# A whole order by hand: five engines in written order, later q casts on POOL, v loads issued by ACT, layer norm in three items

## The chip, the cores and the metric

The kernel runs on one core of a Trainium2 chip. The metric is the device time of one execution in microseconds (us). The engines are PE (TensorE, matrix products), DVE (VectorE), ACT (ScalarE), POOL (GpSimd) and SP (SyncE, here only a DMA issuer). Times of one kernel spread by some 3%. The sets of runs were made on different chips, so a kernel is compared with the kernel before of its own set. A run over 1.5% above the fastest of its kernel in the same set counts as slow and is left out of the ratios. The ratios are the mean time of one kernel's fast runs over that of the other's fast runs of the same rounds, so they are not quite the ratio of the medians that stand beside them. Verdicts use a line of 2%.

## The reference

A decaying linear attention feeds a gated MLP. Shapes: q, k, v are 4 x 8 x 768 x 64 (batch, head, position, head dimension); the MLP has 512 inputs and 1024 hidden values, half gate and half content.

```python
# attention, per batch and head, in blocks of 64 positions
intra = ((q_b @ k_b.T) * Dmask) @ v_b              # Dmask: lam^(i-j) for i >= j
inter = (q_b * lam_pow) @ kv_state
out[block] = intra + inter
kv_state = lam_block * kv_state + (k_b * rev_pow).T @ v_b
# gated MLP on x = out, heads side by side
h = relu(x @ w_in);  u, v = h[..., :512], h[..., 512:]
v_n = (v - mean(v)) / sqrt(var(v) + 1e-6)           # over the last axis
v_s = w_spatial @ v_n + b_spatial[:, None]          # mixes the 768 positions of a batch
y = (u * v_s) @ w_out
```

Each batch can start its spatial product (`w_spatial @ v_n`) only when the attention and the layer norm of all its positions are done. That product is what the text calls **pvs**; the first pvs of each batch is a good milestone.

## The kernel before

The work is cut into 12 steps of 256 positions, three steps for each of the four batches. One step n consists of these items:

```python
load_step(n)   # k, q, v of the step from memory, all issued by SP
cast_step(n)   # kd = k * decay (DVE for n < 3, else POOL); qc = q (ACT); vc = v (POOL); all to bf16
trans_step(n)  # T: PE transposes kd and qc; ACT copies kT, DVE writes qT
scores_step(n) # A: PE scores pam; DVE multiplies the mask: a
kv_step(n)     # K: PE state update pkv; DVE s = decay * s_prev + pkv (through a tile sd)
out_step(n)    # O: PE output pat = state part + a @ v; ACT copies to xT
pv(b, r)       # content half of w_in; relu on ACT (vh); layer norm on DVE and ACT (vn)
pu(b, r)       # gate half of w_in; relu on ACT (uT)
pvs(b, f), po(b, r)   # spatial product and gate; output product and store
```

The order of PE's and POOL's instructions is written by hand. DVE, ACT and SP are ordered by the framework's scheduler. The hand-written loop looks ahead: while step n is put out, step n + 1 is scored, step n + 2 is cast and transposed, and the MLP's products are put between as fill, so that PE has independent work while DVE and ACT finish a link of the attention.

```python
    with tc.manual_schedule(engines={PE, mybir.EngineType.Pool}):
        # ... cast_step(0), win, cast_step(1), spatial and output weights, trans, scores, kv of step 0, trans of step 1
        for n in range(NS):
            if n + 2 < NS:
                cast_step(n + 2)
            if n + 5 < NS:
                load_step(n + 5)
            if n + 1 < NS:
                scores_step(n + 1)
            out_step(n)
            after_out(n)                 # appends pv, pu, pvs, po to the list of fills
            if n + 1 < NS:
                kv_step(n + 1)
            f = fills.get(n, 4 + (n % 3 == 0))
            fill(f // 2)
            if n + 2 < NS:
                trans_step(n + 2)
            fill(f - f // 2)
        fill(len(pend))
```

Of the kernel before, what the change touches and what calls it, by code (L numbers as in the profile page):

```python
# [9 lines left out]
FP32 = mybir.dt.float32  # L10
BF16 = mybir.dt.bfloat16
I32 = mybir.dt.int32
AF = mybir.ActivationFunctionType
ALU = mybir.AluOpType
PE = mybir.EngineType.PE
# [3 lines left out]
def kernel(  # L19
# [12 lines left out]
    nc = tc.nc  # L32
    P = 128
    B, H, S, D = q.shape
    DM = H * D
    DFF = moe_w_in.shape[1]
    DH = DFF // 2
    NBLK = S // P
    NG = H // 2
    NCH = DM // P  # L40
# [16 lines left out]
        return psum.tile(shape, dt, tag="ps", name=name)  # L57


    lam_bc = const.tile([P, H], FP32)  # L60
    nc.scalar.dma_start(out=lam_bc, in_=lam.unsqueeze(0).to_broadcast((P, H)))

    st = {}

    def load_step(n):
        b, r = divmod(n, NR)
        toks = slice(r * T2, (r + 1) * T2)
        q_in = fin.tile([P, H, 2, D], FP32, tag="q_in", name=f"q_in_{n}")
        k_in = fin.tile([P, H, 2, D], FP32, tag="k_in", name=f"k_in_{n}")
        v_in = fin.tile([P, H, 2, D], FP32, tag="v_in", name=f"v_in_{n}")  # L70
        for c in range(2):
            nc.sync.dma_start(out=k_in[:, :, c, :],  # L72
                              in_=k[b, :, toks][:, c * P:(c + 1) * P].rearrange("h p d -> p h d"))
        nc.sync.dma_start(out=q_in.rearrange("p h m d -> p h (m d)"),  # L74
                          in_=q[b, :, toks].rearrange("h (p m) d -> p h (m d)", m=2))
        for c in range(2):
            nc.sync.dma_start(out=v_in[:, :, c, :],  # L77
                              in_=v[b, :, toks][:, c * P:(c + 1) * P].rearrange("h p d -> p h d"))
        st[n] = {"q_in": q_in, "k_in": k_in, "v_in": v_in}

    load_step(0)
    ident = const.tile([P, P], BF16)
    make_identity(nc, ident)

    def iota_f(shape, pattern, base, mult, name):
        ti = const.tile(shape, I32, name=name + "_i")
        nc.gpsimd.iota(ti, pattern=pattern, base=base, channel_multiplier=mult)
        tf = const.tile(shape, FP32, name=name)
        nc.vector.tensor_copy(out=tf, in_=ti)
        return tf  # L90

    krev = iota_f([P, 1], [[0, 1]], P - 1, -1, "krev")

    qpos = iota_f([P, 2, 2, D], [[1, 2], [0, 2], [2, D]], 1, 0, "qpos")

    rel = iota_f([P, 2, D], [[1, 2], [2, D]], 0, -1, "rel")

    win_sb = wpool.tile([P, NCH, DFF], BF16)
    wout_sb = wpool.tile([P, NCH, DM], BF16)
    bsp_bc = wpool.tile([P, S], BF16)  # L100
    wt_sb = wpool.tile([P, NBLK, S], BF16)
    wsp_raw = wpool.tile([P, NBLK, S], BF16)

    def load_win(f0, f1):
        nc.gpsimd.dma_start(out=win_sb[:, :, f0:f1],
                            in_=moe_w_in.rearrange("(g p) f -> p g f", p=P)[:, :, f0:f1])

    load_win(DH, DFF)
    for n in range(1, 4):
        load_step(n)  # L110


    loglam = const.tile([P, H], FP32)
    nc.scalar.activation(out=loglam, in_=lam_bc, func=AF.Ln)
# [3 lines left out]
        nc.vector.tensor_copy(out=logl[rows, :], in_=loglam[rows, hh::2])  # L118
    ldec = const.tile([P, H], FP32)
    nc.scalar.activation(out=ldec, in_=loglam, func=AF.Exp, scale=krev[:, 0:1])  # L120
    lq = const.tile([P, NG, T2], BF16)
    for g in range(NG):
        nc.scalar.activation(out=lq[:, g, :], in_=qpos.rearrange("p m a d -> p (m a d)"),
                             func=AF.Exp, scale=logl[:, g:g + 1])
    l128 = const.tile([P, NG], FP32)
    nc.scalar.activation(out=l128, in_=logl, func=AF.Exp, scale=float(P))
    lm128 = const.tile([P, H], FP32)
    nc.scalar.activation(out=lm128, in_=loglam, func=AF.Exp, scale=-float(P))
    causal = const.tile([P, P], FP32)
    nc.vector.tensor_scalar(out=causal, in0=rel.rearrange("p m d -> p (m d)"), scalar1=0.0,  # L130
                            scalar2=None, op0=ALU.is_ge)
    amask = const.tile([P, 2, 2, 2, P], FP32)
    for h in range(H):
        nc.vector.tensor_scalar(out=amask[:, h // 4, h % 2, (h // 2) % 2, :], in0=causal,
                                scalar1=lm128[:, h:h + 1], scalar2=None, op0=ALU.mult)
    eps_t = const.tile([P, 1], FP32)
    nc.vector.memset(eps_t, 1e-6)
    oo128 = const.tile([P, P], BF16)
    nc.vector.memset(oo128, 1.0 / P)


    xT = {}

    def cast_step(n):
        s = st[n]
        kd = att.tile([P, 2, H, D], BF16, tag="kd", name=f"kd_{n}")
        qc = att.tile([P, 2, H, D], BF16, tag="qc", name=f"qc_{n}")
        vc = att.tile([P, H, 2, D], BF16, tag="vc", name=f"vc_{n}")
        eng = nc.vector if n < NR else nc.gpsimd
        eng.tensor_tensor(out=kd.rearrange("p c h d -> p h c d"), in0=s["k_in"],  # L150
                          in1=ldec.unsqueeze(2).unsqueeze(3).broadcast_to((P, H, 2, D)),
                          op=ALU.mult)
        nc.scalar.activation(out=qc.rearrange("p m h d -> p h m d"), in_=s["q_in"], func=AF.Copy)  # L153
        nc.gpsimd.tensor_copy(out=vc, in_=s["v_in"])  # L154
        s["kd"], s["qc"], s["vc"] = kd, qc, vc

# [112 lines left out]
    def pv(b, r):  # L269
        if r == 0:  # L270
            gmlp_tiles(b)
        x, m = xT[b], gm[b]
        vh, mv, rstd = m["vh"], m["mv"], m["rstd"]
        ps = two_banks([P, 2, DH], f"pv_{b}_{r}")
        for j in range(2):
            for c in range(NCH):
                nc.tensor.matmul(out=ps[:, j], lhsT=x[:, r, c, j * P:(j + 1) * P],  # L277
                                 rhs=win_sb[:, c, DH:DFF], start=(c == 0), stop=(c == NCH - 1))
        pair = slice(2 * r, 2 * r + 2)
        nc.scalar.activation(out=vh[:, pair, :], in_=ps, func=AF.Relu)  # L280
        for t in (2 * r, 2 * r + 1):
            nc.vector.bn_stats(out=m["st6"][:, t, :], in_=vh[:, t, :])  # L282
            nc.vector.bn_aggr(out=mv[:, t, :], in_=m["st6"][:, t, :])
        nc.scalar.activation(out=rstd[:, pair], in_=mv[:, pair, 1], func=AF.Sqrt,
                             bias=eps_t[:, 0:1])
        nc.vector.reciprocal(out=rstd[:, pair], in_=rstd[:, pair])
        for t in (2 * r, 2 * r + 1):
            nc.vector.tensor_scalar(out=m["vn"][:, t, :], in0=vh[:, t, :],  # L288
                                    scalar1=mv[:, t, 0:1], scalar2=rstd[:, t:t + 1],
                                    op0=ALU.subtract, op1=ALU.mult)  # L290
# [45 lines left out]
        nc.scalar.activation(out=wt_sb[:, s:s + 2, :], in_=ps[:, :, 0:S], func=AF.Copy)  # L336


    pend = []

    def fill(n):
        for _ in range(min(n, len(pend))):
            pend.pop(0)()

    def after_out(n):
        b, r = divmod(n, NR)
        pend.append(lambda: pv(b, r))
        if r == 0:
            pend.append(lambda: pu(b, 0))
        if r == NR - 1:  # L350
            pend.append(lambda: pu(b, 1))
            pend.append(lambda: pu(b, 2))
            if b == 0:
                pend.extend([lambda s=s: wt_piece(s) for s in (0, 2, 4)])
            pend.extend([lambda f=f: pvs(b, f) for f in range(NCH)])
            pend.extend([lambda i=i: po(b, i) for i in range(NR)])

    with tc.manual_schedule(engines={PE, mybir.EngineType.Pool}):
        cast_step(0)
        load_win(0, DH)  # L360
        cast_step(1)
        nc.gpsimd.dma_start(out=wsp_raw, in_=moe_w_spatial.rearrange("(a p) s -> p a s", p=P))
        nc.gpsimd.dma_start(out=bsp_bc, in_=moe_b_spatial.unsqueeze(0).to_broadcast((P, S)))
        nc.gpsimd.dma_start(out=wout_sb, in_=moe_w_out.rearrange("(t p) f -> p t f", p=P))
        trans_step(0)
        scores_step(0)
        kv_step(0)
        trans_step(1)
        load_step(4)
        fills = {0: 1, 1: 2, 2: 5}  # L370
        for n in range(NS):
            if n + 2 < NS:
                cast_step(n + 2)
            if n + 5 < NS:
                load_step(n + 5)
            if n + 1 < NS:
                scores_step(n + 1)
            out_step(n)
            after_out(n)
            if n + 1 < NS:  # L380
                kv_step(n + 1)
            f = fills.get(n, 4 + (n % 3 == 0))
            fill(f // 2)
            if n + 2 < NS:
                trans_step(n + 2)
            fill(f - f // 2)
        fill(len(pend))


# [28 lines left out]
```

## Time and profile before

| | before |
|---|---|
| time, median (range) of 3 runs | 188.25 us (187.67 to 188.35) |
| span of the profiled run | 186.7 us |
| PE busy, idle | 145.7, 41.0 us |
| DVE, ACT, POOL busy | 103.4, 89.1, 34.8 us |
| first pvs of the four batches at | 63.7, 102.1, 136.8, 166.0 us |

The page's first part gives busy time, share and instruction count of each engine. Its row PEclk gives the clock granted to TensorE in 40 slices of the span, in tenths:

```profile
PE 145.7 (78%) x1540; PEld 96.5 (52%) x1540; DVE 103.4 (55%) x191; ACT 89.1 (48%) x98; POOL 34.8 (19%) x35
PEclk9999996975999979999999999999999999999999
```

PE's clock falls in slices 6 to 14 only (counted from 0), that is before 70 us. The view of waits lists what an engine waited for (us in total, times, longest). Its first lines for PE are the holes of the first stage:

```profile
PE pt L163 <- DVE kd L150: 15.5, 2, 14.3
PE pkv L207 <- POOL vc L154: 8.1, 1, 8.1
```

The first is the start, before any data is there. The second is the wait for v of step 2.

### The profile page before, as it was taken

What the parts mean: (1) busy time and instruction counts of PE and PEld (TensorE: products, weight loads), DVE (VectorE), ACT (ScalarE), POOL (GpSimd) and SP (SyncE); (2) the same over time, 40 slices, a digit from 0 to 9 for tenths busy, and PEclk for the clock granted to TensorE, in tenths of its full rate; (3) what the DMA queues carried; (4) which work ended last, traced back from release to release, by engine and by line L of the source; (5) the groups of instructions that cost most, each with busy time, mean ns of one, the idle gap of its engine ahead of it and who ended that gap; (6) DMA issues with size and microseconds to landing.
All of it is one profiled execution on the core that took longest, in us unless ns stands there. A gap on an engine that the chain in (4) does not pass through costs nothing.

```text
span 186.7 us, 3638 instructions
## 1 busy us (share of the span) xinstructions
PE 145.7 (78%) x1540; PEld 96.5 (52%) x1540; DVE 103.4 (55%) x191; ACT 89.1 (48%) x98; POOL 34.8 (19%) x35
## 2 busy tenths in 40 slices
PE   0005677507979779999997999999799999999980
PEld 0005563305649556655776665575676646565430
DVE  1029993705399853542989747169884722564400
ACT  4244324712677942268775613666722157660051
POOL 4004060006245344060606005020000000000000
PEclk9999996975999979999999999999999999999999
DMA  4999969999999999999998900530000027000035
GB/s 98 218 211 252 205 161 184 199 212 232 199 241 248 200 239 238 221 225 222 330 254 195 252 8 0 208 133 4 0 0 4 2 79 262 0 0 4 0 132 205
DMA packets 68337, 28.36 MB, mean 152 GB/s; under 512 B 50528, under 2 KB 65248, under 8 KB 68320
## 3 DMA queue, kind: packets, MB, share of 16 engines
q1 hardware_dynamic: 65664, 25.17, 56.5%
q0 software_dynamic: 2512, 2.95, 9.6%
q8 instruction: 12, 0.20, 0.5%
q14 instruction: 5, 0.04, 0.1%
q10 hardware_dynamic: 144, 0.00, 0.0%
HBM read 24.78 MB, written 6.29 MB: 166 GB/s over the span
## 4 chain that ended last, share of the span: by engine, by line
PE 54%; SPq 13%; DVE 11%; ACT 9%; DMA 9%; issue 2%; POOL 1%; ACTq 0%; POOLq 0%
PE pvs L307 17%; PE po L322 11%; DMA v_in<-in_v_dram 9%; PE pv L277 8%; PE pu L297 7%; SPq L77 6%; SPq L72 5%; PE pt L163 4%; DVE a L192 3%; PE pvs L309 3%; SPq L74 3%; DVE st L282 3%; ACT vh L280 2%; ACT wt_sb L336 2%; DVE vn L288 2%
## 5 line engine op out<-in xcount | busy, mean ns | idle before, releaser
L307 PE MATMUL pvs<-wt_sb,vn 128*128 128x384 bf16 x192 | 37.8, 331 | 2.1 <-ACT wt_sb L336 2.0
L192 DVE TENSOR_TENSOR a<-pam,amask 128x1024 bf16<-128x1024 f32 x24 | 28.5, 1210 | 6.0 <-PE pam L189 6.0
L154 POOL CAST vc<-v_in 128x1024 bf16<-128x1024 f32 x12 | 12.9, 1074 | 84.0 <-DMA v_in<-in_v_dram 42.7
L252 ACT ACTIVATE xT<-pat 128x1024 bf16<-128x1024 f32 x12 | 15.8, 1320 | 23.7 <-PE pat L249 23.6
L307 PEld LDWEIGHTS <-vn 128*128 128x128 bf16 x192 | 18.9, 99 | 14.9 <-issue 2.5
L297 PE MATMUL pu<-xT,win_sb 128*128 128x256 bf16 x192 | 24.4, 285 | 1.9 <-DVE a L192 1.9
L311 DVE TENSOR_TENSOR gT<-pvs,uT 128x768 bf16<-128x768 f32 x16 | 15.3, 958 | 18.2 <-PE pvs L309 18.1
L277 PE MATMUL pv<-win_sb,xT 128*128 128x512 bf16 x96 | 24.2, 400 | 1.2 <-ACT xT L252 1.2
L322 PE MATMUL po<-wout_sb,gT 128*128 128x512 bf16 x96 | 21.9, 379 | 1.5 <-DVE a L192 1.1
L297 PEld LDWEIGHTS <-win_sb 128*128 128x128 bf16 x192 | 19.2, 102 | 5.7 <-issue 1.8
L153 ACT ACTIVATE qc<-q_in 128x1024 bf16<-128x1024 f32 x12 | 12.7, 1055 | 19.0 <-DMA q_in<-in_q_dram 19.0
L325 ACT ACTIVATE o<-po 128x1024 f32<-128x1024 f32 x12 | 12.3, 1025 | 19.0 <-PE po L322 19.0
L282 DVE BATCH_NORM_STATS2 st<-vh 128x6 f32<-128x512 bf16 x24 | 15.6, 682 | 10.4 <-ACT vh L280 10.3
L163 PE MATMUL pt<-ident,kd 128*128 128x128 bf16 x96 | 8.6, 242 | 15.5 <-DVE kd L150 15.5
L170 DVE TENSOR_TENSOR qT<-pt,lq 128x1024 bf16<-128x1024 bf16 x12 | 8.2, 684 | 18.5 <-ACT kT L168 18.5
L150 POOL TENSOR_TENSOR kd<-k_in,ldec 128x1024 bf16<-128x1024 f32 x9 | 17.1, 1897 | 6.1 <-DMA k_in<-in_k_dram 6.1
L168 ACT ACTIVATE kT<-pt 128x1024 bf16<-128x1024 bf16 x12 | 12.2, 1021 | 11.2 <-PE pt L163 11.2
L280 ACT ACTIVATE vh<-pv 128x1024 bf16<-128x1024 f32 x12 | 12.3, 1024 | 8.8 <-PE pv L277 8.8
L163 PEld LDWEIGHTS <-kd 128*128 128x128 bf16 x96 | 7.2, 110 | 17.4 <-DVE kd L150 15.7
L277 PEld LDWEIGHTS <-xT 128*128 128x128 bf16 x96 | 9.5, 102 | 11.7 <-issue 1.7
L322 PEld LDWEIGHTS <-gT 128*128 128x128 bf16 x96 | 9.2, 98 | 11.9 <-issue 1.0
L299 ACT ACTIVATE uT<-pu 128x1024 bf16<-128x1024 f32 x12 | 12.2, 1020 | 5.9 <-PE pu L297 5.8
(52 smaller groups left out, 146.2 us busy)
## 6 DMA issues: line engine op xcount, KB each, us to landing
k_in<-in_k_dram SPq DMA_DIRECT2D x24, 256.0 KB, 5.8
q_in<-in_q_dram SPq DMA_DIRECT2D x12, 512.0 KB, 6.1
v_in<-in_v_dram SPq DMA_DIRECT2D x24, 256.0 KB, 6.0
out_dram<-o SPq DMA_DIRECT2D x12, 512.0 KB, 3.4
wsp_raw<-in_moe_w_spatial_dram POOLq DMA_DIRECT2D x1, 1152.0 KB, 11.3
win_sb<-in_moe_w_in_dram POOLq DMA_DIRECT2D x2, 512.0 KB, 8.4
wout_sb<-in_moe_w_out_dram POOLq DMA_DIRECT2D x1, 512.0 KB, 14.8
bsp_bc<-in_moe_b_spatial_dram POOLq DMA_DIRECT2D x1, 192.0 KB, 11.7
```

The source lines that it names most:

```text
L150: eng.tensor_tensor(out=kd.rearrange("p c h d -> p h c d"), in0=s["k_in"], in1=ldec.unsqueeze(2).unsqueeze(3).broadcast_to((P, H, 2, D)), ...
L154: nc.gpsimd.tensor_copy(out=vc, in_=s["v_in"])
L163: nc.tensor.transpose(out=pt[:, j, g, c * P:(c + 1) * P], in_=src[:, c, 2 * g:2 * g + 2, :].rearrange("p h d -> p (h d)"), identity=ident)
L192: nc.vector.tensor_tensor(out=a_sb[:, i].rearrange("p h g c x -> p (h g) c x"), in0=pam.rearrange("p h g c x -> p (h g) c x"), in1=amask[: ...
L252: nc.scalar.activation(out=xT[b][:, r].rearrange("p g (c d m) -> p (g c) m d", c=2, m=2), in_=po.rearrange("p g c (m d) -> p (g c) m d", m ...
L277: nc.tensor.matmul(out=ps[:, j], lhsT=x[:, r, c, j * P:(j + 1) * P], rhs=win_sb[:, c, DH:DFF], start=(c == 0), stop=(c == NCH - 1))
L280: nc.scalar.activation(out=vh[:, pair, :], in_=ps, func=AF.Relu)
L282: nc.vector.bn_stats(out=m["st6"][:, t, :], in_=vh[:, t, :])
L297: nc.tensor.matmul(out=ps[:, f], lhsT=win_sb[:, c, f * P:(f + 1) * P], rhs=x[:, r, c, :], start=(c == 0), stop=(c == NCH - 1))
L307: nc.tensor.matmul(out=ps[:, i, 0:HW_], lhsT=m["vn"][:, s, f * P:(f + 1) * P], rhs=wt_sb[:, s, cols], start=(s == 0), stop=False)
L311: nc.vector.tensor_tensor(out=m["gT"][:, f, :].rearrange("p (i x) -> p i x", i=2), in0=ps[:, :, 0:HW_], in1=m["uT"][:, f, :].rearrange("p ...
L322: nc.tensor.matmul(out=ps[:, j], lhsT=gT[:, c, t * P:(t + 1) * P], rhs=wout_sb[:, c, :], start=(c == 0), stop=(c == NCH - 1))
```

## The change

The intent is a front without the hole at v of step 2 and full control of what runs when. All five engines follow one hand-written text of items. v goes out on ACT's hardware queue, so that it need not queue behind k and q; the weights go out one after another when they are needed; q casts of steps 3 and up go to POOL; layer norm is split into l0 (statistics, DVE), l1 (square root, ACT) and l2 (reciprocal and vn, DVE), which can be placed apart.

```diff
+    def load_v(n):
         for c in range(2):
-            nc.sync.dma_start(out=v_in[:, :, c, :], ...
+            nc.scalar.dma_start(out=v_in[:, :, c, :], ...
+    ctx.enter_context(tc.manual_schedule(engines={
+        PE, mybir.EngineType.Pool, mybir.EngineType.Activation, mybir.EngineType.DVE,
+        mybir.EngineType.SP}))
+    for n in range(4):
+        load_step(n)                     # k and q of four steps first on SP
+    load_v(0)                            # ... load_v(1) follows the tables on ACT
 ...
-        nc.scalar.activation(out=qc.rearrange("p m h d -> p h m d"), in_=s["q_in"], func=AF.Copy)
+        if n == 0:
+            nc.vector.tensor_copy(out=qo, in_=s["q_in"])
+        elif n < NR:
+            nc.scalar.activation(out=qo, in_=s["q_in"], func=AF.Copy)
+        else:
+            nc.gpsimd.tensor_copy(out=qo, in_=s["q_in"])
 ...
-    # the loop with lookahead and fills
+    run("""
+        c:0 win T:0 mask A:0 K:0 O:0 pv:0:0 l0:0:0 pu:0:0 l1:0:0
+        c:1 lv:2 T:1 l2:0:0 A:1 K:1 O:1
+        c:2 wsp lv:3 T:2 pv:0:1 pu:0:1 l0:0:1 l1:0:1 A:2 l2:0:1 K:2 O:2
+        wout lk:4 c:3 lv:4
+        pv:0:2 l0:0:2 pu:0:2 wt:0 l1:0:2 wt:2 l2:0:2 wt:4
+        lk:5 c:4 lv:5 T:3 pvs:0:0 pvs:0:1 A:3 K:3 lk:6 c:5 lv:6 pvs:0:2 T:4 pvs:0:3 po:0:0
+        A:4 O:3 K:4 po:0:1 lk:7 c:6 lv:7 T:5 po:0:2 pv:1:0
+        ...
+    """)
+    for n in range(2 * NR, NS):          # a = batch before that of step n
+        run(f"A:{n + 1} O:{n} K:{n + 1}")            # guards left out
+        if r == 0:
+            run(f"l2:{a}:2 pvs:{a}:0 pvs:{a}:1 {nxt} pvs:{a}:2 pvs:{a}:3")
+        ...
```

Each engine takes its instructions in the order of this text. `T:1` stands for the transposes of step 1, `l2:0:1` for the normalization of the second third of batch 0, `lk` and `lv` for the loads.

## The prediction

> **What bounds the kernel now.** I first read the page's slices, then the chain of waits that ended last, then the timeline of the first 60 us, and last the busy time by stretch.
>
> ```profile
> PE   0005677507979779999997999999799999999980
> DMA  4999969999999999999998900530000027000035
> ```
> One digit is 4.67 us. TensorE (PE) is full from about slice 15 (70 us) on; before that it has holes, while the DMA engines are full. So there are two stages. The table by stretch (columns: stretch, its length, busy us and instructions of PE, PEld, DVE, ACT and POOL, granted PE clock, DMA share, GB/s) puts numbers on them:
> ```profile
> 35.00:40.00 5.00, 0.02 (x2) 0.00 (x0) 2.40 (x5) 2.89 (x3) 0.00 (x0) 1.00 1.19 202
> 60.00:70.00 10.00, 7.47 (x104) 5.59 (x102) 7.22 (x9) 7.49 (x7) 3.48 (x3) 0.86 1.12 219
> 90.00:100.00 10.00, 9.38 (x119) 6.76 (x117) 9.29 (x24) 7.93 (x11) 2.87 (x3) 1.00 1.08 273
> 140.00:150.00 10.00, 9.63 (x105) 6.04 (x103) 5.92 (x7) 2.33 (x2) 0.00 (x0) 1.00 0.01 2
> ```
> Adding PE's column over the stretches: 37.7 us busy in 0 to 70 (32.3 idle), 106.5 in 70 to 180 (3.5 idle), 1.5 in the last 6.7 (5.2 of tail: last copy, last store). Only the first stage has much to give. The chain of waits (start, us, what) names its largest piece:
> ```profile
> 25.91 15.96 DMA v_in<-in_v_dram
> 41.91 0.08 issue
> 42.00 1.05 POOL vc L154
> 43.09 0.43 PE pkv L207 x6
> ```
> PE stood still because the state update of step 2 waited for v of step 2. The timeline shows what that load ran beside:
> ```profile
> 25.44 0.83 POOL L362 DMA_DIRECT2D wsp_raw<-in_moe_w_spatial_dram  x1
> 26.26 0.56 POOL L363 DMA_DIRECT2D bsp_bc<-in_moe_b_spatial_dram  x1
> 26.54 10.03 SPq L72 DMA_DIRECT2D k_in<-in_k_dram  x2
> 26.81 0.76 POOL L364 DMA_DIRECT2D wout_sb<-in_moe_w_out_dram  x1
> 42.00 1.04 POOL L154 CAST vc<-v_in 128x1024 bf16<-128x1024 f32 x1 [14.43 <-DMA v_in<-in_v_dram]
> 43.09 0.43 PE L207 MATMUL pkv<-vc,kd 128*64 128x64 bf16 x8 [8.07 <-POOL vc L154]
> ```
> Spatial weights, bias and output weights (1152 + 192 + 512 KB as landed) went out at 25.4 to 27.6 and landed 11.3 to 14.8 us after issue (page, DMA issues). From 26 to 42 the DMA moved about 3.1 MB at 177 to 243 GB/s, of which those weights are 1.9 MB; v of step 2 got through at 41.9. None of them is used before 59. The v load is also last in SP's queue, behind k and q of its step and backpressure of up to 10 us for two issues.
>
> [...] So v on ACT's queue [...] lets v pass the k and q queued ahead. [...] two vn took 2.09 us at 44.09 beside a POOL kd of 1.90 at 43.81, and 0.73 for two at 54.68 with POOL idle. [...] granted clock 0.50 in 30 to 32; eight pv took 3.57 us at 29.76, 1.89 at 47.72. [...] for vc, 1.04 us; I take 1.05 for a qc cast there.
>
> **The change, part by part.**
> Steady state. PE's work is unchanged. From the warm pieces of the chain, one step costs transposes 0.89 + scores 0.55 + attention output 1.13 + state 0.25 + pv 1.73 + pu 1.85 = 6.40; a batch adds pvs, four tiles of 2 x (0.97 + 0.16) = 9.04, and po 3 x 1.73 = 5.19. A batch is 33.4. Before, first po to first po takes 34.76 and 34.57 us (79.82, 114.58, 149.15), so it idles 1.2 a batch; hand ordering can save at most some 3.5 us there, and I credit none.
> Casts: 9 x 1.06 = 9.5 us leave ACT for POOL, whose step becomes 1.90 + 1.05 + 1.04 = 4.0 of about 11.5 us; both lie beside PE. Cost: [...] up to about 1 us of DVE delay a step, mostly hidden as DVE is 55% busy.
> v issues: 24 move from SP to ACT. An unobstructed SP issue took 0.43 us, the obstructed ones up to 5.10. About 1 us a step on ACT cancels the cast gain; hidden later, dangerous in the first 30 us.
> Layer-norm pieces as separate items: same instructions, other places in the queues, no work removed. Early Sqrt table: the 1.28 us load at 36.4 moves to the start.
> Front. I lay it out anew; estimates from durations above:
> - k0, q0 (SP) and v0 (ACT) are 1.57 MB. With data from about 2.3 us at 215 GB/s, v0 lands near 7, q0 near 10. Before, the first win half shared this time and the first transposes began at 14.33. Now: qc on DVE to 11, transposes (cold) 11 to 13, kT 1.02, qT 0.69, scores, mask 1.66 and two a of 1.2 in a row, output and xT 1.3: xT at about 20.5. Before it was 27.3: 7 us sooner.
> - win is issued by POOL only after v0's cast, at about 9 to 10.5; its halves took 8.1 and 8.7 us alone, so both land near 18 and 24. pv of step 0 runs 20.5 to 24 and pu 24 to 27.5, cold. So late win costs little.
> - ACT then does uT, sqrt, qc1 to about 29, and issues v2. Step 1: transposes 30, kT, qT, scores 32.5, a, output, xT at 35.5; v2, issued 29 to 30 and alone with SP at half of 215 GB/s, needs 4.9 us and lands about 35. POOL casts it and issues the spatial weights at 36.5.
> - Step 2: cast 36.5, transposes, pv and pu of step 1 to 41, scores, output, xT at 44.5; pv, pu of step 2 to 48; spatial weights land 36.5 + 11.3 = 48; wt pieces and evictions (1.46 each) to 53.
> - So the first pvs starts at about 53 instead of 66.49. But before had by then also done the attention of step 3 and the scores of step 4, some 4 us of PE, which after still owes.
> Sum: 53 + first batch's pvs and po 14.2 + 3 x 33.4 + idle 3 x 1.2 + tail 5.2 = 176.2. Span to reported time adds 1.6 (188.25 against 186.7): 177.8. I take 177.5; put otherwise, 13.5 us of front minus 4 us of work owed, a little under 10 us.
>
> **Rivals.** (a) ACT stalls at its v issues as SP did. For: 5.10 us for one v issue on SP, and SP runs full just when v1 is issued (9 us). Against: ACT's queue is empty then. Two stalls of 3 to 4 us before 35 us would give 184 to 186. (b) Contention only moves: win beside v1 and k1, spatial weights beside v3, [...] so step 1 or 3 waits. For: bytes needed by 53 us (4 x 1.57 MB and the weights, 9.2 MB) take 45 us at 205 GB/s, so there are only some 5 us of slack. Against: v3 is needed only after the first pvs. If step 3 waits 4 us: 182. (c) Strict order on five engines opens bubbles in the steady state: a tile of PSUM is reused after four, and one misplaced eviction stops PE. 0.5 us a step over nine steps: 182. (d) Better than laid out: PE stays warm in step 0 (saves 3.4 us), and the hand order takes half the 3.5 us of idle: 172. An engine other than PE becoming the bound is unlikely: DVE is 103.4 us, ACT 89.1.
>
> **Range and chances.** Working sum 177.5; (d) reaches to 171, any of (a) to (c) to about 184, two together pass 185. Range 170.5 to 185. The 2% line is 184.5: faster 0.87, within 2% 0.09, slower 0.04 (only if strict order stalls badly throughout, which 3.5 us of idle now gives no ground for).
>
> **What would show each step.** First transposes before 12 us, xT of step 0 near 20; no PE wait on vc of step 2 above 2 us; wsp issued after 33; first pvs at 50 to 56; batch period 33.5 to 35 us; POOL qc near 1.05 us, POOL busy 44; ACT busy near 80. Wrong if v issues on ACT take more than 2 us each, if the front is as long as before, or if the batch period exceeds 35.5 us.

## The result, and the profile after

The kernel after took 204.03 us median (202.75 to 208.66, 4 runs, one of them slow) against 187.96 us (186.13 to 188.35) for the kernel before in the same rounds: ratio 1.086, 95% interval 1.0766 to 1.0954. It is slower by some 16 us where 10 less had been predicted. The outputs are correct.

The page of the kernel after, first part, then PE, granted clock and DMA in 40 slices of 5.08 us:

```profile
PE 150.2 (74%) x1528; PEld 96.9 (48%) x1540; DVE 107.4 (53%) x191; ACT 78.8 (39%) x89; POOL 44.8 (22%) x44
...
PE   0134663368379799999692899999829999999980
...
PEclk9999997558759999999999699999966999999997
DMA  4999999999960900499999600697000005200035
```

ACT lost and POOL gained what was predicted. PE starts earlier (digits in slices 1 and 2, counted from 0) and then stays half empty up to slice 10, at 56 us. New holes stand in slice 21 (107 us) and slice 29 (147 us), each with a dip of the clock right behind; before had no clock dip in its steady state and no digit under 7 there. PE is idle 203.3 - 150.2 = 53.1 us instead of 41.0, and busy 4.5 us longer for the same products, which goes with the lower granted clock (0.917 in the mean against 0.963): 12.1 + 4.5 = 16.6 us, the whole difference of the spans.

By milestones (start of the first pvs of each batch):

| stage, us | before | after | difference |
|---|---|---|---|
| start to first pvs | 63.7 | 65.2 | +1.5 |
| first pvs of batch 0 to that of batch 1 | 38.4 | 43.4 | +5.0 |
| batch 1 to 2 | 34.7 | 40.2 | +5.5 |
| batch 2 to 3 | 29.2 | 33.8 | +4.6 |
| first pvs of batch 3 to end | 20.7 | 20.7 | 0.0 |

Of the +5.0, about 3.6 us are attention products that before had already done ahead of its first pvs (scores, state and output of step 3, transposes, scores and state of step 4, by the durations in the prediction's chain).

Two cautions. The prediction (66.49) and the expectations (67.7) count the first pvs from the point after its wait for the transposed weights; this text counts its first matmul, 63.7 and 65.2. And one profile is one execution: a second one of the same kernel (after_ctl below, span 201.1 us) has its first pvs at 62.6, and then stages of 43.1, 40.9, 33.8 and 20.6 us. So the first stage varies by 2.6 us from run to run; the later stages agree.

**The front.** The waits of PE in the kernel after:

```profile
PE pt L187 <- DVE kd L168: 15.5, 3, 9.3
PE pat L266 <- DVE s L243: 5.9, 2, 3.5
PE pvs L342 <- DVE vn L323: 5.4, 2, 3.0
...
PE pvs L342 <- DVE a L216: 3.0, 2, 1.8
```

The wait of the state update for v of step 2 (8.1 us) is gone, as wanted. Others took its place, all four of those shown on DVE. The last of them, pvs behind the mask product a, is no wait for data, since pvs doesn't read a: it can only be for one of the four PSUM tiles (PE's output memory) that all products share. The chain that ended last, followed through this stretch (start, us, what), shows why:

```profile
33.15 2.27 DVE a L216 x2
...
36.31 1.20 DVE sd L242
...
37.87 4.45 DVE kd L168
...
42.37 1.89 PE pt L187 x16
...
50.11 2.24 DVE a L216 x2
...
57.98 2.70 PE pv L301 x6
```

It is one attention step after the other. Mask product, state, cast, transposes, pv, statistics, mask product again: the links of the chain don't overlap, because the text finishes step 1 before it casts and transposes step 2. The kernel before looked ahead by a step. The kd of step 2 also took 4.45 us in this execution against 1.2 for the same work elsewhere. The timeline (start, us, engine, line, what, and in brackets the idle time before it) shows what it lay beside:

```profile
37.87 4.44 DVE L168 TENSOR_TENSOR kd<-k_in,ldec 128x1024 bf16<-128x1024 f32 x1
37.99 0.56 POOL L154 DMA_DIRECT2D bsp_bc<-in_moe_b_spatial_dram  x1
...
38.53 0.76 POOL L157 DMA_DIRECT2D wout_sb<-in_moe_w_out_dram  x1
...
39.29 1.93 POOL L168 TENSOR_TENSOR kd<-k_in,ldec 128x1024 bf16<-128x1024 f32 x1
...
42.37 1.03 PE L187 MATMUL pt<-ident,kd 128*128 128x128 bf16 x8 [4.41 <-DVE kd L168]
```

DVE's kd did not end until POOL had issued its weights and finished its own kd of step 3 (at 41.22). But this isn't so in every execution. In the control run of the same kernel, kd of step 2 started 0.7 us before the first weight issue instead of 0.7 us behind it, and was short:

```profile
36.92 1.83 DVE L168 TENSOR_TENSOR kd<-k_in,ldec 128x1024 bf16<-128x1024 f32 x1
37.62 0.82 POOL L153 DMA_DIRECT2D wsp_raw<-in_moe_w_spatial_dram  x1
```

That run lost as much against the kernel before (ratio 1.0948). So the long kd goes with the later first pvs of the profiled run, but it isn't what the loss rests on.

**The batch boundaries.** The timeline around the first pvs of batch 2:

```profile
147.59 2.32 DVE L216 TENSOR_TENSOR a<-pam,amask 128x1024 bf16<-128x1024 f32 x2
...
151.59 0.16 DVE L321 RECIPROCAL rstd<-rstd 128x2 f32<-128x2 f32 x1
151.79 0.73 DVE L323 TENSOR_SCALAR vn<-vh,mv,rstd 128x512 bf16<-128x512 bf16 x2
152.26 0.82 PE L342 MATMUL pvs<-wt_sb,vn 128*128 128x384 bf16 x2 [2.34 <-DVE vn L323]
```

The last third of vn is what pvs needs. Its square root had run at 147.70, but DVE first did the mask product and four state instructions of the next step, because `l2:{a}:2` stands behind A, O and K in the text. PE stopped for 2.34 us and then went on at a low clock, 0.50 in the mean from 152 to 156 us. The table by stretch (length, busy us and instructions of PE, PEld, DVE, ACT, POOL, granted clock, DMA share, GB/s) shows both kinds of loss, a stretch of the front and one of the boundary:

```profile
50.00:60.00 10.00, 4.67 (x38) 2.51 (x39) 3.92 (x8) 1.73 (x3) 3.88 (x3) 0.68 1.08 215
150.00:160.00 10.00, 7.74 (x47) 4.51 (x48) 4.23 (x9) 0.83 (x1) 0.00 (x0) 0.70 0.01 2
```

Ten microseconds at a granted clock of 0.70 with a DMA share of 0.01: the loss at this boundary has nothing to do with transfers.

### The profile page after: what moved, and what is told of

It reads as the page before. It is cut to its first block, busy times and chain, and to the rows that moved or that the text cites. A ratio compares the mean times of both kernels' runs of the same rounds, so it can differ in the third digit from the quotient of the medians.

```text
span 203.3 us, 3632 instructions
## 1 busy us (share of the span) xinstructions
PE 150.2 (74%) x1528; PEld 96.9 (48%) x1540; DVE 107.4 (53%) x191; ACT 78.8 (39%) x89; POOL 44.8 (22%) x44
## 4 chain that ended last, share of the span: by engine, by line
PE 43%; DVE 23%; SPq 11%; DMA 10%; ACT 7%; issue 2%; POOL 1%; ACTq 0%; DVEq 0%; POOLq 0%
PE pvs L342 16%; PE po L357 9%; SPq L68 8%; DVE a L216 7%; PE pv L301 6%; DMA k_in<-in_k_dram 5%; DMA q_in<-in_q_dram 4%; SPq L70 4%; PE pu L332 3%; PE pt L187 3%; DVE st L310 3%; PE pvs L344 3%; DVE kd L168 3%; DVE vn L323 3%; DVE gT L346 2%; DVE sd L242 2%
## 5 line engine op out<-in xcount | busy, mean ns | idle before, releaser
L342 PE MATMUL pvs<-wt_sb,vn 128*128 128x384 bf16 x192 | 40.2, 345 | 10.1 <-DVE vn L323 5.4
L342 PEld LDWEIGHTS <-vn 128*128 128x128 bf16 x192 | 19.4, 102 | 24.8 <-issue 7.8
L310 DVE BATCH_NORM_STATS2 st<-vh 128x6 f32<-128x512 bf16 x24 | 16.2, 675 | 24.6 <-ACT vh L304 24.6
L301 PE MATMUL pv<-win_sb,xT 128*128 128x512 bf16 x89 | 26.4, 433 | 3.7 <-ACT xT L276 2.8
L168 POOL TENSOR_TENSOR kd<-k_in,ldec 128x1024 bf16<-128x1024 f32 x9 | 17.2, 1910 | 43.4 <-DMA k_in<-in_k_dram 43.4
L332 PE MATMUL pu<-xT,win_sb 128*128 128x256 bf16 x192 | 23.2, 277 | 0.0
L301 PEld LDWEIGHTS <-xT 128*128 128x128 bf16 x96 | 10.1, 109 | 15.7 <-issue 5.0
L304 ACT ACTIVATE vh<-pv 128x1024 bf16<-128x1024 f32 x12 | 12.2, 1021 | 12.6 <-PE pv L301 11.8
L187 PEld LDWEIGHTS <-kd 128*128 128x128 bf16 x96 | 6.7, 105 | 18.7 <-DVE kd L168 16.0
L357 PEld LDWEIGHTS <-gT 128*128 128x128 bf16 x96 | 9.0, 97 | 12.1 <-DVE gT L346 1.8
L266 PE MATMUL pat<-qT,s 64*64 64x128 bf16 x160 | 8.0, 238 | 8.8 <-DVE s L243 5.9
## 6 DMA issues: line engine op xcount, KB each, us to landing
win_sb<-in_moe_w_in_dram POOLq DMA_DIRECT2D x2, 512.0 KB, 10.7
```

What stands on the lines that cost most here:

```text
L168: eng.tensor_tensor(out=kd.rearrange("p c h d -> p h c d"), in0=s["k_in"], in1=ldec.unsqueeze(2).unsqueeze(3).broadcast_to((P, H, 2, D)), ...
L187: nc.tensor.transpose(out=pt[:, j, g, c * P:(c + 1) * P], in_=src[:, c, 2 * g:2 * g + 2, :].rearrange("p h d -> p (h d)"), identity=ident)
L301: nc.tensor.matmul(out=ps[:, j], lhsT=x[:, r, c, j * P:(j + 1) * P], rhs=win_sb[:, c, DH:DFF], start=(c == 0), stop=(c == NCH - 1))
L310: nc.vector.bn_stats(out=m["st6"][:, t, :], in_=vh[:, t, :])
L332: nc.tensor.matmul(out=ps[:, f], lhsT=win_sb[:, c, f * P:(f + 1) * P], rhs=x[:, r, c, :], start=(c == 0), stop=(c == NCH - 1))
L342: nc.tensor.matmul(out=ps[:, i, 0:HW_], lhsT=m["vn"][:, s, f * P:(f + 1) * P], rhs=wt_sb[:, s, cols], start=(s == 0), stop=False)
```

## The experiments

The theory after the traces: two placements in the hand-written order (no lookahead in the first batch; the last normalization behind the next step's work) make most of the loss. The rivals: strict order as such on DVE, ACT and SP; the v loads on ACT; the stores in front of later loads on SP; the q casts on POOL, beside which DVE can run slower (two vn took 2.09 us beside a POOL kd and 0.73 with POOL idle, in the kernel before). "Before" is the median of the kernel before in the same set of runs. The profiled executions of a_lk7, a_best2, a_vint, a_vint_fkl and a_fkl were slow ones, so their milestones are a little late.

### 1. Is it strict order itself?

**a_auto**: the kernel after, with DVE, ACT and SP ordered by the framework again.

```diff
     ctx.enter_context(tc.manual_schedule(engines={
-        PE, mybir.EngineType.Pool, mybir.EngineType.Activation, mybir.EngineType.DVE,
-        mybir.EngineType.SP}))
+        PE, mybir.EngineType.Pool}))
```

> The changed kernel, but DVE, ACT and SP are put in order by the framework's scheduler again, as in the kernel before; only PE and POOL keep the hand order. Theory H (the strict hand order of DVE, ACT and SP is what loses: an op that waits holds up ready ones behind it): at least 12 of the 16 us come back, 185 to 192 us, and the first pvs moves from 67.7 to about 55. Theory C (contention and late data are the loss: casts on POOL blocking DVE, v on ACT's queue, spatial weights late): 198 to 205 us. Theory L (k and q loads stuck behind stores in SP's order): about 195, and POOL's wait of 18 to 20 us for k is gone.

Measured: 213.7 us (213.23 to 215.61), before 185.72; ratio 1.1555. First pvs at 77.7 us. All three theories missed.

**b_hand**: the kernel before, with all five engines in the order of its program text.

```diff
-    with tc.manual_schedule(engines={PE, mybir.EngineType.Pool}):
+    with tc.manual_schedule(engines={PE, mybir.EngineType.Pool, mybir.EngineType.DVE,
+                                  mybir.EngineType.Activation, mybir.EngineType.SP}):
```

> The kernel before, with one thing added: DVE, ACT and SP in the order in which the program was written, instead of the scheduler's. Theory H: 194 to 205 us, with more idle time of PE between 70 and 180 us than the 3.5 us of before. Theory C and theory L: 186 to 190 us, the same as before.

Measured: 213.7 us (210.55 to 214.33); ratio 1.1445, also outside both ranges. PE waited 13.2 us for xT in pu alone.

Neither half of the question has a simple answer. The text of the kernel after is bad for the scheduler too (213.7), and the text of the kernel before, never written for strict order, loses some 26 us under it. So these two runs don't separate strict order from the text. That strict order need not cost 16 us is shown only by a_vint_fkl below, which keeps it.

### 2. The suspects one at a time

**after_ctl**: the kernel after once more, as a control beside later runs.

```diff
(no edit)
```

> The changed kernel itself once more, as the measure for the next two on the same chip: 202 to 206 us by every theory.

Measured: 202.94 us (201.12 to 203.32), before 187.03; ratio 1.0948. The loss stands.

**a_lk7**: loads of k and q of step 7 ahead of the first store on SP's queue.

```diff
-        ... pvs:0:2 T:4 pvs:0:3 po:0:0
-        A:4 O:3 K:4 po:0:1 lk:7 c:6 lv:7 T:5 po:0:2 pv:1:0
+        ... pvs:0:2 T:4 pvs:0:3 lk:7 po:0:0
+        A:4 O:3 K:4 po:0:1 c:6 lv:7 T:5 po:0:2 pv:1:0
```

> The changed kernel, but the k and q loads of step 7 are put on SP ahead of the first output store instead of behind the second one. Theory L: POOL's wait for k at 74 to 93 us shrinks to a few us, ACT's issue of v at 103 us is no longer held, 196 to 199 us. Theories H and C: the k wait shrinks all the same, but PE's idle time stays and the time stays within 2 us of 204.

Measured: 205.59 us (203.47 to 208.24); ratio 1.1008. No gain. The gaps of DMA between 61 and 81 us in the kernel after (slices 12, 14 and 15) were real, and POOL stood up to 20 us behind them. With the edit POOL's kd of step 7 began at 72.53 instead of 92.76 us, but PE didn't depend on it.

**a_qcact**: q casts of all later steps on ACT again.

```diff
-        elif n < NR:
-            nc.scalar.activation(out=qo, in_=s["q_in"], func=AF.Copy)
         else:
-            nc.gpsimd.tensor_copy(out=qo, in_=s["q_in"])
+            nc.scalar.activation(out=qo, in_=s["q_in"], func=AF.Copy)
```

> The changed kernel, but all q casts from step 1 on are on ACT as in the kernel before (step 0 stays on DVE). Theory C [...]: DVE's slow ops shrink (the kd cast of 4.44 us at 37.9 to about 2.5), 198 to 201 us. Theory H: 202 to 206 us, since ACT then waits in strict order for q too.

Measured: 206.82 us (206.31 to 207.43); ratio 1.1165. The casts on POOL aren't the cause; by the ratios they help by some 2%.

**a_kd2pool**: kd of step 2 on POOL, which removes the 4.45 us instruction from DVE. The first ranges expected are for the case that this instruction is a term of the front's loss.

```diff
-        eng = nc.vector if n < NR else nc.gpsimd
+        eng = nc.vector if n < 2 else nc.gpsimd
```

> The changed kernel, but the kd cast of step 2 is on POOL (ahead of v's cast and the spatial-weight issues) instead of DVE, where it took 4.44 us beside POOL's issues and casts. [...] transposes of step 2 start at 37 to 39 us instead of 42.4, the first pvs 2 to 5 us earlier, 199 to 202 us. If another op of DVE is caught in its place, or step 2 is held by something else: transposes may move, the first pvs stays within 1.5 us of 67.7, 203 to 206 us.

Measured: 204.23 us (201.95 to 206.37), before 186.97; ratio 1.0993. Transposes of step 2 began at 37.96 instead of 42.37 and its xT at 52.71 instead of 55.78, yet the time did not change within the spread (the profiled span was 200.1 us). The control says why: there, without the edit, they began at 38.81 and 52.78. Against it the first pvs came 0.6 us earlier (62.0 and 62.6). The long kd of one profile was not a part of the loss that other runs share.

**a_l2**: the last normalization of a batch ahead of the next step's mask product, at the two boundaries where it stood behind it.

```diff
-        run(f"A:{n + 1} O:{n} K:{n + 1}")
+        run(("l2:{a}:2 " if r == 0 else "") + f"A:{n + 1} O:{n} K:{n + 1}")
 ...
-            run(f"l2:{a}:2 pvs:{a}:0 pvs:{a}:1 ...")
+            run(f"pvs:{a}:0 pvs:{a}:1 ...")
```

> The changed kernel, but at the two later batch boundaries the last layer-norm item (reciprocal and vn of the batch's last step) stands in DVE's order before the masked scores of the next step instead of behind them. Theory P (the loss sits in the written order: PE reaches pvs and finds vn behind scores and state updates on DVE): PE's waits of 3.0 and 2.3 us for vn fall below 1 us, the half-clock matmuls after them go too, and 5 to 9 us come back: 195 to 199 us. Theory D (the loss is late data and contention): at most 2 us, 202 to 206 us.

Measured: 198.69 us (197.21 to 199.66), before 186.94; ratio 1.0781. The two stages that it touches took 37.3 and 30.7 us instead of 40.2 and 33.8, so 2.9 and 3.1 us less. This is the only single edit of the kernel after that gained clearly: 6.0 us in these two stages, 4.0 us by the mean of the fast runs (198.6, and 202.6 for after_ctl).

**a_front**: steps 1 and 2 looked ahead as in the kernel before (cast and transposes of the next step before the MLP's products of this one); v still on ACT.

```diff
-        c:0 win T:0 mask A:0 K:0 O:0 pv:0:0 l0:0:0 pu:0:0 l1:0:0
-        c:1 lv:2 T:1 l2:0:0 A:1 K:1 O:1
-        c:2 wsp lv:3 T:2 pv:0:1 pu:0:1 l0:0:1 l1:0:1 A:2 l2:0:1 K:2 O:2
+        c:0 win T:0 mask A:0 K:0 O:0 c:1 lv:2 pv:0:0 T:1 l0:0:0 pu:0:0 A:1 l1:0:0
+        K:1 c:2 O:1 wsp lv:3 T:2 l2:0:0 pv:0:1 A:2 l0:0:1 pu:0:1 K:2 l1:0:1 O:2 l2:0:1
```

> The changed kernel, but in the first batch each step's casts, transposes and scores are written ahead of the step before's pv and pu, as in the kernel before, instead of behind them. Theory P: transposes of step 1 start before 26 us (29.4 now), of step 2 near 34 (42.4 now), the first pvs moves from 67.7 to 56 to 60, and the time falls by 6 to 11 us: 193 to 198 us. Theory D: the front still waits for v and the weights, first pvs after 64 us, 201 to 206 us.

Measured: 205.16 us (202.96 to 205.61); ratio 1.1091. No gain at all, first pvs at 64.5 us. Transposes of step 1 came at 24.90 as expected, those of step 2 at 42.51. This contradicted the theory that the front's order is a large term, and asked for a reason. In this trace ACT was idle for 6.64 us ahead of its relu of step 0, which stood behind the issue of v of step 2, and the state's DVE instruction, 0.41 us when alone, took 3.44 beside POOL's weight issues and kd:

```profile
37.04 3.44 DVE L242 TENSOR_TENSOR sd<-s,l 128x256 f32<-128x256 bf16 x1
```

**a_vsp**: v on SP's queue, issued at the same places of the text.

```diff
-            nc.scalar.dma_start(out=v_in[:, :, c, :],
+            nc.sync.dma_start(out=v_in[:, :, c, :],
```

> The changed kernel, but the v loads are issued by SP, at the same places of the written order, instead of by ACT. Theory D, with v on ACT as the harm (ACT held at the issues): 198 to 202 us. Theory P: no gain; v then queues behind four steps of k and q in the front, so step 1 comes later, 205 to 212 us.

Measured: 211.57 us (210.15 to 212.1); ratio 1.145. Worse: behind k and q of four steps, v of step 1 came late, and PE waited 11.6 us for vc in one state update, where the kernel after shows no wait of PE for vc. So v on ACT does pass k and q at the start, as the prediction said.

### 3. The order edits together, v on ACT

**a_best2**: lookahead, kd of step 2 on POOL, the normalization, the step 7 loads, the weights issued ahead of step 2's casts, and v of step 2 issued right behind the first transposes.

```diff
-        c:0 win T:0 mask A:0 K:0 O:0 pv:0:0 ...
+        c:0 win T:0 lv:2 mask A:0 K:0 O:0 c:1 pv:0:0 T:1 l0:0:0 pu:0:0 A:1 l1:0:0
+        wsp wout K:1 c:2 O:1 lv:3 T:2 l2:0:0 pv:0:1 A:2 l0:0:1 pu:0:1 K:2 l1:0:1 O:2 l2:0:1
 (and the edits of a_kd2pool, a_l2, a_lk7)
```

> The changed kernel with four edits of its order together: layer norm ahead of the scores at the batch boundaries, steps 1 and 2 written ahead of the pv and pu before them, kd of step 2 on POOL with the weights issued before that step, v of step 2 issued early, and k and q of step 7 ahead of the stores. Theory P [...]: first pvs at 54 to 60 us, batch periods below 38 us, 183 to 190 us. If the front is bound by the bytes that SP loads ahead: first pvs above 63, 192 to 197 us.

Measured: 202.09 us (201.33 to 204.5); ratio 1.0826. A miss. ACT got v of step 2 out late, and the xT of step 0 behind it came at 24.06 us instead of 20.44:

```profile
14.26 9.74 ACTq L79 DMA_DIRECT2D v_in<-in_v_dram  x2
```

The line merges two issues. The first took 0.38 us; the second did not start before 23.58 and took 0.43, so 9.74 us from the start of one to the end of the other.

### 4. The same with v off ACT

**a_vint**: v issued by SP right behind k and q of its own step; ACT issues no loads of the inputs but lam. Nothing else moves.

```diff
         st[n] = {"q_in": q_in, "k_in": k_in}
+        load_v(n)
 ...
-            nc.scalar.dma_start(out=v_in[:, :, c, :],
+            nc.sync.dma_start(out=v_in[:, :, c, :],
 (all lv items leave the text)
```

> The changed kernel, with one part undone: v is loaded by SP directly behind k and q of its step, as in the kernel before, and ACT issues no loads. If v on ACT's queue is a term of the loss (v of steps 1 and 2 issued late by ACT's order, weights issued behind v's cast): first pvs at 58 to 62 us, 196 to 200 us. If not: first pvs at 63 to 68, 202 to 206 us.

Measured: 204.08 us (201.85 to 205.8); ratio 1.0943, first pvs at 65.0. Alone, moving v changes nothing in the time, though xT of step 0 came at 18.9 us instead of 21.7: in this text the front waits for DVE's links either way (PE's longest waits are 10.1 us in two for the state s and 9.1 us in three for kd, both of DVE).

**a_vint_f**: a_vint with the lookahead of a_front.

```diff
 (a_vint, and)
+        c:0 win T:0 mask A:0 K:0 O:0 c:1 pv:0:0 T:1 l0:0:0 pu:0:0 A:1 l1:0:0
+        K:1 c:2 O:1 wsp T:2 l2:0:0 pv:0:1 A:2 l0:0:1 pu:0:1 K:2 l1:0:1 O:2 l2:0:1
```

> The changed kernel with v on SP's queue behind k and q of its step, and steps 1 and 2 looked ahead; kd of step 2 stays on DVE, the last normalization of a batch stays behind the next step's work, loads of step 7 stay. If the front's order is the larger term: 193 to 197 us with first pvs at 56 to 58 and later batches as in the changed kernel (43, 40, 34). If the lookahead gives nothing without the other edits: 202 to 205 us and first pvs at 63 or later.

Measured: 194.37 us (193.62 to 194.51), before 186.16; ratio 1.0433. First pvs at 54.1 us instead of 65.0, xT of step 2 at 45.2; later stages 42.4, 42.0 and 33.8, near those of the kernel after.

**a_vint_fkl**: a_vint_f with kd of step 2 on POOL, the normalization of a_l2 and the loads of a_lk7. The first ranges expected are for the case that these edits cover the whole loss.

```diff
 (a_vint_f, and the edits of a_kd2pool, a_l2, a_lk7)
```

> The kernel of the run before this one, and with it steps 1 and 2 written ahead of the pv and pu before them, kd of step 2 on POOL, the layer norm ahead of the scores at the batch boundaries, and step 7's loads ahead of the stores. [...] first pvs at 52 to 58 us and 183 to 190 us. If something else bounds the front (bytes, or the half clock): first pvs above 60 and 192 to 197 us.

Measured: 188.02 us (185.68 to 188.65), before 187.03; ratio 1.0119, interval 0.9998 to 1.0239. Some 15 us are back, by this ratio and after_ctl's 1.0948 of the same set. In its PE row (slices of 4.67 us) the two late holes are shallower, digits 4 and 5 in slices 19 and 29 where the kernel after has 2 and 2:

```profile
PE   0433973964988999998496999999859999999980
```

**a_fkl**: the same order edits, v on ACT as in the kernel after, v of step 2 issued behind the cast of step 1.

```diff
 (kernel after, and the edits of a_front, a_kd2pool, a_l2, a_lk7)
```

> The same four order edits as the run that recovered the loss (steps 1 and 2 looked ahead, kd of step 2 on POOL, last normalization of a batch ahead of the next mask product, loads of step 7 ahead of the first store), but v stays on ACT's hardware queue as in the changed kernel. Theory queue (ACT is held at its v issues while SP's queue is backed up, so the order edits pay only when v leaves ACT): 195 to 203 us, with an ACT issue of v of several us in the first 30 us and first pvs at 60 or later. Theory order only (the queue of v does not matter once the order is mended): 186 to 191 us, first pvs at 54 to 57.

Measured: 194.37 us (192.7 to 198.0), before 186.16; ratio 1.0411, interval 1.0295 to 1.0526. It falls just below the range of the theory that the queue matters (195 to 203) and clearly above that of the other (186 to 191). First pvs at 60.0 instead of 54.4; the later stages agree with a_vint_fkl to within 2 us each. So with the order mended, v on ACT costs 5 to 6 us by the ratios. The two profiled runs, both slow ones, differ by 9.3 us, of which 5.6 lie ahead of the first pvs. (The reading below is of an order of events, not of a time difference.) The chain of a_fkl says how:

```profile
17.53 11.05 DMA k_in<-in_k_dram
...
28.60 0.37 ACTq L79
...
29.02 1.02 ACT vh L304
...
38.80 17.45 DMA k_in<-in_k_dram
...
56.27 0.37 ACTq L79
...
56.69 1.02 ACT vh L304
```

Twice in this trace a v issue on ACT started 0.02 us after a k load on SP had landed (28.60 after 28.58 and 56.27 after 56.25, by the first two numbers of each k line), and ACT's relu stood behind it (29.02 and 56.69). The pv that these relus read had ended at 25.35 and 54.46, so by this trace the two holds cost ACT 3.6 and 2.2 us. What ties a v issue to such a load, the traces don't show. In the kernel after, v of step 2 was held too: its second half went out at 29.47, 0.02 us after the other half of k of step 3 had landed. But ACT was busy with the q cast until 29.85 and lost nothing. Where the edits moved the issue forward, to where the front needs it, the hold stood in front of ACT's relu (a_front, a_fkl) or its copy to xT (a_best2). That is at least a part of why a_front alone and a_best2 gained nothing. No run took away the hold alone.

### 5. What is left of the idea in the kernel before

**b_wlate**: spatial, bias and output weights issued behind the v cast of step 2, as the prediction's reading of the hole suggested.

```diff
-        (three weight loads behind cast_step(1))
         for n in range(NS):
             if n + 2 < NS:
                 cast_step(n + 2)
+            if n == 0:
+                (the three weight loads)
```

> The kernel before, with one thing changed: spatial weights, bias and output weights are issued by POOL after the cast of v of step 2 instead of before it. If the record's reading of the chain is right (those weights hold up v of step 2 by up to 16 us), PE's wait of 8.1 us for v in step 2 falls below 2 us and the time to 180 to 186 us. If v would have been late anyway (SP's own queue of k and q), the wait stays above 5 us and the time stays within 2 us of before.

Measured: 189.06 us (188.57 to 189.81); ratio 1.0246. The 8.1 us wait for v of step 2 vanished, and two others came: 4.3 us for v of step 3, which now was loaded beside the weights (the prediction's rival (b), in the kernel before), and 6.4 us for the xT of step 2, which stood behind the q cast of step 4 in the order that the scheduler gave ACT.

```profile
45.95 0.64 PE L207 MATMUL pkv<-vc,kd 128*64 128x64 bf16 x16 [4.31 <-POOL vc L154]
...
50.71 1.06 ACT L153 ACTIVATE qc<-q_in 128x1024 bf16<-128x1024 f32 x1 [9.96 <-DMA q_in<-in_q_dram]
```

**b_qcpool**: q casts of steps 3 and up on POOL, weights where they were. The first rival expected is that DVE runs slower beside the added work on POOL.

```diff
-        nc.scalar.activation(out=qc.rearrange("p m h d -> p h m d"), in_=s["q_in"], func=AF.Copy)
+        if n < NR:
+            nc.scalar.activation(out=qo, in_=s["q_in"], func=AF.Copy)
+        else:
+            nc.gpsimd.tensor_copy(out=qo, in_=s["q_in"])
```

> The kernel before, with only the q casts from step 3 on moved from ACT to POOL. The record holds that they lie beside PE in either place: within 2 us of before, POOL busy near 44 and ACT near 80 us. A rival: [...] 189 to 193 us. A second rival: ACT no longer waits for q in its order (19.0 us in the kernel before), 182 to 185 us.

Measured: 188.13 us (184.23, 188.31, 188.57, 187.94). No ratio came of it, since only one run counted as fast. Inconclusive.

**b_wlq**: both.

```diff
 (b_wlate and b_qcpool)
```

> The kernel before, with the late spatial weights of the last set, and the q casts from step 3 on moved to POOL. With the late weights alone xT of step 2 stood 10 us behind the q cast of step 4 in ACT's order. If that cast was all that held it: xT of step 2 near 43 instead of 51.7, first pvs at 54 to 60 instead of 68, 176 to 183 us. If the bytes themselves are late (the next wait is for q and v of steps 3 and 4): first pvs above 64, 184 to 190 us.

Measured: 183.59 us (182.18 to 184.91); ratio 0.9843, interval 0.9603 to 1.0083. First pvs at 59.8 instead of 63.7.

**b_best**: both, and the two halves of w_in issued behind the first v cast.

```diff
-    load_win(DH, DFF)                    # ahead of the loads of steps 1 to 3
 ...
         cast_step(0)
+        load_win(DH, DFF)
         load_win(0, DH)
 (and the edits of b_wlq)
```

> The kernel before with three parts of the change's idea: q casts from step 3 on on POOL, spatial weights, bias and output weights issued after v of step 2, and both halves of w_in issued after v of step 0 instead of the first half at once. If bytes bound the front, the start moves (transposes at 11 to 12 instead of 14 us) but the first pvs stays near 60 us: 180 to 185 us. If w_in arrives too late for pv of step 0: 184 to 188 us.

Measured: 182.43 us (181.94 to 184.05); ratio 0.9875, interval 0.9795 to 0.9955. It beats both kernels, by 1.25% over the kernel before; that is less than the 2% line, and the recorded verdict is unclear.

```profile
PE   0047337970698799999979999999799999999880
```

First pvs at 60.0, and no digit under 7 between slice 11 and the last.

## Why the prediction was wrong

**Right.** Step 0 of the front ran as laid out: xT ended at 21.7 (20.5 predicted), pu of step 0 at 27.7 (27.5), the transposes of step 1 began at 29.37 (30), v of step 2 was cast at 36.19 and the weights issued at 37.17 (36.5 for both). POOL's q cast took 1.04 us undisturbed (mean 1.165), POOL was busy 44.8 us (44), ACT 78.8 (80). The early table load and the late w_in cost nothing (the load took 1.28 us at 7.98, and ACT was idle for 3.32 us ahead of its next copy, at 12.80; pv of step 0 waited 1.40 us for xT and not for w_in). The wait for v of step 2 went away. v passed k and q at the start (a_vsp). The last-pvs-to-end stage is the same.

**The step that failed first: "Step 2: cast 36.5, transposes, pv and pu of step 1 to 41, scores, output, xT at 44.5".** It took the front from durations of PE's work with one allowance for each link. Measured: xT of step 1 at 39.3 (35.5), transposes of step 2 at 42.37 (37), xT of step 2 at 57.1 (44.5), first pvs at 65.2 (53). Three things were left out. With no lookahead the links on DVE follow one another: two mask products of 2.3 us together, the state, statistics, again two mask products. kd of step 2 took 4.45 us beside POOL's work in the profiled run; with 1.83 us in the control the first pvs still came at 62.6. And PE, which had little work, ran at a granted clock of 0.68 from 50 to 60 us; the eight pv of step 2 took about 3.3 us at 0.52 (57.15 to 60.60), where eight pv of the kernel before took 1.89 at 1.00 (at 47.72). Removing the first of these, with v on SP, brought xT of step 2 to 45.2 and first pvs to 54.1: the predicted 44.5 and 53 were nearly in reach, but not with this text.

**The second: "hand ordering can save at most some 3.5 us there, and I credit none" and rival (c) at "182".** The steady state wasn't left as it was. The predicted batch was 33.4 + 1.2 = 34.6 us, three of them 103.8; the three stages took 43.4 + 40.2 + 33.8 = 117.4, so 13.6 us more. The prediction never read where `l2:{a}:2` stands in DVE's order. a_l2 shows about 3 us for each of two boundaries. The mechanism was rival (c)'s, one misplaced item under strict order; its size, 0.5 us a step or 4.5 in all, was too small. Rival (c) thought of PSUM tiles; the item that a_l2 moved is another, though waits for such tiles are there too (pvs behind a mask product, 3.0 us in two). No single run takes the other 7.6 us of the 13.6 apart.

**The sum.** Predicted span 176.2, measured 203.3, so 27.1 us off: front 65.2 - 53 = 12.2, three batches 13.6, last batch 20.7 - (14.2 + 5.2) = 1.3. Two readings of the prediction were off without entering this sum: the 13.5 us of front in its cross-check start from 66.49, where the trace has the first pvs at 63.7 (so 10.7); and the halves of win did not take 8.1 and 8.7 us alone, but beside loads of k, q and v.

**Rival (a)**, a stall of ACT at its v issues, cost nothing in the front of the kernel after (each issue took 0.37 to 0.60 us, and the hold ahead of v of step 2 lay beside a q cast). But a stall was there, and it bit as soon as the order was mended: a_fkl against a_vint_fkl, 5 to 6 us. Whether it was the full queue that the prediction thought of, no trace shows: the two held issues of a_fkl took 0.37 us each, once a k load had landed. Its "lets v pass the k and q queued ahead" held only in part: against v at the same places on SP it did (PE waited 11.6 us for vc in a_vsp), but the second half of v of step 2 went out only when half of k of step 3 had landed (28.60 us in a_fkl, 29.47 in the kernel after).

**The gain from the weights.** The reading that the weights delayed v of step 2 was right (b_wlate took the wait away), but to subtract that wait was not: the next ones, 4.3 us for v of step 3 and 6.4 us behind a late q cast on ACT, stood right behind it.

**How the 16 us divide**, by the ratios: with v on SP, lookahead is worth 1.0943 - 1.0433 = 5.1%, 9 to 10 us; the normalization, kd of step 2 and the step 7 loads another 3.1%, about 6 us, and by a_l2 most of that is the normalization (in the profiles the two later stages lose 4.7 and 4.6 us while the stage from batch 0 to 1 grows by 3.3). With v on ACT the same edits together give only 1.0948 - 1.0411 = 5.4%, 10 us.

**Open.** a_vint_fkl has its first pvs at 54.4, 9.3 us ahead of the kernel before, and ends at the same time: its first pvs-to-pvs stage takes 45.7 us instead of 38.4, of which 3.6 are work owed. Between 85 and 95 us its DVE was busy 9.79 of 10 us and PE 6.60, so I suspect DVE there, but no run tested it. Strict order on five engines with all these edits was not shown to beat the kernel before. The share of kd of step 2 and of the step 7 loads in the last 6 us was not separated with v on SP. And DVE instructions beside POOL's weight issues came out both ways: a kd took 1.23 us there in the kernel before (at 26.27) and 1.22 in a_vint_f (at 31.65), but an sd, 0.41 us when alone, took 3.44 in a_front and 3.51 in a_fkl, and a kd 4.44 in the kernel after, each until after the end of the POOL kd that followed the issues. What makes the difference, no run shows.

## What to carry to other kernels

When an order is rewritten by hand, follow every engine's queue and not only PE's: for each link of the chain ask what stands ahead of it on DVE and ACT, above all at the boundaries between batches, and keep the lookahead that the old order had. A wait that is removed is worth only its distance to the next one, so look for the second-longest wait before promising the first. Before a load is given to a computing engine, look in the trace at what its issue waits for: in a_fkl two v issues that started 0.02 us after a k load had landed kept ACT's relu back by 3.6 and 2.2 us.
